# Attention loop of a fused attention, soft-MoE and feed-forward kernel: order of a pair's steps, one q/k buffer, and the slot step of the last batch

## The chip, the cores and the metric

The kernel runs on one core of a Trainium2 chip. Its time is device microseconds, from the runs of the kernel on that core. All data are float32 in memory.

## The reference, cut to what matters

Causal attention over 4 batches, 12 heads, 448 positions and 64 dimensions; its output, as 1792 tokens of 768, goes through a soft mixture of 8 experts with 4 slots each, and that through a feed-forward layer whose activation is h cos h.

```python
# attention: q, k, v are (4, 12, 448, 64)
scores = scale * np.matmul(q, k.transpose(0, 1, 3, 2))
scores = np.where(mask, -1000000000.0, scores)          # causal
scores = scores - np.max(scores, axis=-1, keepdims=True)
attn = np.exp(scores)
attn = attn / (np.sum(attn, axis=-1, keepdims=True) + 1e-09)
x = np.matmul(attn, v)                                   # then (1792, 768)
# soft MoE: phi (768, 32), w1 (8, 768, 1024), w2 (8, 1024, 768)
logits = x @ phi
d = exp(logits - logits.max(0)); d /= d.sum(0) + 1e-09   # over all tokens
slot_input = d.T @ x                                     # (32, 768)
for e in range(8):
    slot_out[e] = np.maximum(slot_input[e] @ w1[e], 0.0) @ w2[e]
c = exp(logits - logits.max(1)); c /= c.sum(1) + 1e-09   # over the 32 slots
y = c @ slot_out
# feed-forward: w_in (768, 2048), w_out (2048, 768)
h = y @ w_in
out = (h * np.cos(h)) @ w_out
```

## The kernel before

It has three stages. The first runs attention and the slots' softmax; the second runs the experts on the 32 slot rows and streams all of `w1` and `w2`; the third is the feed-forward layer, laid out by a planner at build time. The change touches the first stage and the way from it into the second.

**Pairs and iterations.** Two heads make a pair; a batch has 6 pairs, the kernel `NPAIR` = 24. `pair_step(t)` (line 450) is one iteration of a software pipeline, called for t = 0 to 27 under `tc.manual_schedule()`. There the order of instructions on each engine is the order of the program text; numbers of `PRI` act only outside such blocks. Iteration t computes the scores and exponentials of pair t, transposes the normalised scores of pair t-1 and multiplies them with the values, and transposes the result x of pair t-2.

**One pair.** The scores of a head are split in query blocks: c = 0 (448 key columns), 1 (320), 2 (192) and 3 (64 columns, both heads' last block together). `qk_mm` (line 284, matmuls at L292 and, for c = 3, L287) writes c = 0 of head j to bank j, c = 1 and 2 to bank 2 + j, and c = 3 to the last 64 columns of bank 0, an iteration ahead. `score` (L303) adds the mask on VectorE, takes the row minimum and writes to SBUF; the closure it returns is the exponential on ScalarE (L305) with its row sum. `recip` (L312, L313) and `norm` (L322) normalise, on VectorE and GpSimd by `CFG["norm"]`. `t_a` and `t_b` (transposes at L325) turn one head's weights into banks `TA` and `TB`; `ev_t` (L176) copies each bank to SBUF, all four on ScalarE. `pv` (L355 to L368) multiplies with the values into bank `OB`; `ev_o` (L176, `xts<-bank`) copies x out. `x_t` (L376) transposes x into bank `TA`, and `ev_x` (L178) copies that to `xk` on VectorE.

**Slot work of a batch b.** With bo = t - 6b: `phi_round` in iterations 5 and 7 adds up the slots' logits of six pairs in bank `MB` (L387), and `be_logits` (L392) copies them out. In iteration 8 `be_rep` (L396) spreads them over partitions, `be_d` (L401 to L411) makes the running softmax over tokens, `be_dk` transposes it (L325, L417), and `be_u(b, 0)` (L439, L445) adds the first three pairs' part of d.T x to `uacc`. In iteration 9 `be_tok` (L422 to L432) makes the softmax over slots and `be_u(b, 1)` adds the other three pairs. So the slot work falls on t mod 6 = 5, 1, 2 and 3 once the first batch is done.

**From the loop to the experts.** For the last batch `be_u(3, 0)` is in t = 26 and `be_u(3, 1)` in t = 27. After the loop, outside the manual block, `uacc` is scaled by the softmax's sum (L571 to L573), six matmuls with `rep` (L575) make `slotT` (L576), and the expert loop begins (matmuls at L733 and L748). `be_tok(3)` is written inside the expert loop; the scheduler may place it.

**Buffers and loads.** Large SBUF tiles come from a ring of `NSLOT` = 26 slots of 1 MB: two q/k buffers of two pairs each, two of scores, `pts`, `xts`, two `xk`, and the rest for pieces of the experts' weights, of which there are 48. All loads are issued on SP in program order, and SP waits there until the target is free. At the end of iteration t come `load_raw(t + 3)` for q and k, `load_v(t + 1)`, and up to 18 weight pieces, one in most iterations; `CFG["PL"]` adds pieces from t = 21 on as slots of the attention stage come free. The expert loop issues a further piece for each that it has read. Values of odd pairs lie in the end of an `xk` slot, of even pairs in others.

Of the kernel before, what the change touches and what calls it, by code (L numbers as in the profile page):

```python
# [27 lines left out]
NSLOT = 26  # L28
# [3 lines left out]
LD = False  # L32
CFG = {'rm': 2,
        'PL': {21: 1, 23: 2, 24: 2, 25: 1, 27: 2},
        'ev': 'AAAA',
# [118 lines left out]
def moe_stack_kernel(ctx: ExitStack, tc: tile.TileContext, qk, v, cst, phi, w1, w2, w_in, w_out, out):  # L154
# [36 lines left out]
    qks = [slot(f"qk{i}") for i in range(2)]  # L191
# [3 lines left out]
    xks = [slot(f"xk{i}") for i in range(2)]  # L195
# [26 lines left out]
    def QK(p):  # L222
        return qks[p // 2 % 2][:, (p % 2) * 960:(p % 2) * 960 + 960]
# [126 lines left out]
    @pr(lambda i: f"ev{i}")  # L350
    def ev_t(i):
        copy(CFG["ev"][i], PT(i), (TA, TB)[i % 2])

# [65 lines left out]
    @pr("tok")  # L419
    def be_tok(b):  # L420
        for r in range(4):
            PE.matmul(MB[0:112, 128 + 32 * r:160 + 32 * r], lhsT=ltr[:, 112 * r:112 * r + 112], rhs=rep[:, 0:32],  # L422
                      start=True, stop=True)
# [4 lines left out]
        ACT.activation(ek, ek, AF.Exp)  # L428
        DVE.tensor_reduce(st[0:112, 20:24], ek, axis=AX.X, op=ALU.add)
# [4 lines left out]
    @pr("u")  # L434
    def be_u(b, half):
        for i in range(3):
            p = b * NPB + 3 * half + i
            for r in range(4):
                PE.matmul(MB[32 * r:32 * r + 32, 128 * i:128 * i + 128], lhsT=dk[0:112, r, :], rhs=XK(p)[:, r, :],  # L439
                          start=True, stop=True)  # L440
        u = uacc[:, 384 * half:384 * half + 384]
        if b == 0:
            DVE.tensor_copy(u, MB[:, 0:384])
        else:
            DVE.scalar_tensor_tensor(u, u, st[:, 9:10], MB[:, 0:384], op0=ALU.mult, op1=ALU.add)  # L445


    NPRE = NSLOT - 8

    def pair_step(t):  # L450
# [7 lines left out]
        def sc(j, c, p=t):  # L458
            if p < NPAIR:
                ex[j, c] = score(p, j, c)  # L460

        def e(j, c):
            if (j, c) in ex:
# [52 lines left out]
        if 8 in bo:  # L516
            be_dk(bo[8])
        if prv:
            pv(p1)
# [12 lines left out]
        if 9 in bo:  # L532
# [16 lines left out]
    with tc.manual_schedule():  # L549
        load_raw(0)  # L550
        SP.dma_start(cs, cst)
        load_raw(1)
        load_v(0)
        SP.dma_start(phs, phi)
        load_raw(2)
# [7 lines left out]
        for t in range(NPAIR + 4):  # L563
# [3 lines left out]
    slotT = phs  # L567
# [3 lines left out]
    DVE.tensor_scalar(st[:, 40:41], st[:, 11:12], 1e-9, None, op0=ALU.add)  # L571
    DVE.reciprocal(st[:, 41:42], st[:, 40:41])
    DVE.tensor_scalar(uacc, uacc, st[:, 41:42], None, op0=ALU.mult)  # L573
    for i in range(6):
# [465 lines left out]
```

## Time and profile before

| | us |
|---|---|
| median of 3 runs | 581.81 |
| lowest, highest | 581.11, 583.5 |
| the profiled execution | 580.56 |
| its span, first to last instruction | 578.8 |
| first scores of the first pair | 5.42 |
| first scores of the last pair | 194.86 |
| first expert matmul | 223.73 |

The profile is that of one execution, with times in us from the span's start. PE is TensorE's matmuls, PEld its weight loads, DVE VectorE, ACT ScalarE, POOL GpSimd, and SPq the queue on which the loads are issued. A line of a timeline merges instructions of one kind that follow each other; the bracket at its end tells how long the engine was idle before it and what ended that. A line of a stretch has the stretch and its length, each engine's busy time with its count of instructions, the granted clock of TensorE as a share of 2.4 GHz, the DMA engines' busy share and GB/s. Some records of instructions can be missing, so that counts of equal stretches differ a little.

### The profile page before, as it was taken

How to read it: one execution, taken by the hardware profiler on the slowest of the kernel's cores; microseconds unless marked ns; L12 is line 12 of the kernel's file. 1: busy time of each engine (PE TensorE's matmuls, PEld its weight loads, DVE VectorE, ACT ScalarE, POOL GpSimd, SP SyncE). 2: the span in 40 equal slices, each digit the busy share in tenths (PEclk: the TensorE clock that was granted, in tenths of full speed). 3: DMA queues.
4: the chain of work that ended last, by engine and by line, in shares of the span. 5: the costliest groups of instructions: out<-in, count | busy, mean ns of one | idle time of the engine just before them, and what ended most of it. 6: DMA issues, size and time to landing. Idle time of an engine off the chain costs nothing.

```text
span 578.8 us, 10216 instructions
## 1 busy us (share of the span) xinstructions
PE 529.0 (91%) x3772; PEld 379.2 (66%) x3772; DVE 347.0 (60%) x879; ACT 329.9 (57%) x762; POOL 174.8 (30%) x209
## 2 busy tenths in 40 slices
PE   5999989999998969998676999899999999999997
PEld 2666666666666634333164878687877777888997
DVE  4566576657657632300176887799588996534532
ACT  4888768868876831011066666565655745443552
POOL 1332332232233210000024346263533734322231
PEclk9999999999999996999796999999999999999999
DMA  7364716554570896999954143333324210202201
GB/s 242 135 246 174 251 65 240 178 197 180 178 251 24 315 370 253 421 418 421 418 199 163 54 165 109 110 110 109 110 109 171 102 53 5 109 2 109 110 1 54
DMA packets 23953, 100.26 MB, mean 173 GB/s; under 512 B 2656, under 2 KB 6624, under 8 KB 17760
## 3 DMA queue, kind: packets, MB, share of 16 engines
q1 hardware_dynamic: 23904, 99.63, 46.4%
q8 instruction: 29, 0.48, 0.3%
q14 instruction: 20, 0.16, 0.1%
HBM read 94.11 MB, written 5.51 MB: 172 GB/s over the span
## 4 chain that ended last, share of the span: by engine, by line
PE 50%; DMA 17%; ACT 15%; DVE 13%; issue 4%; POOL 1%; SPq 0%; ACTq 0%; DVEq 0%; POOLq 0%
PE bank L831 7%; PE bank L830 7%; DMA w<-in_w_dram 7%; PE bank L832 7%; DMA zraw<-in_w_in_dram 5%; ACT pts L176 5%; PE bank L292 5%; ACT p L305 4%; PE bank L325 4%; DMA zraw<-in_w_out_dram 4%; PE bank L360 3%; PE bank L376 2%; PE bank L362 2%; PE bank L733 2%; DVE zscr L811 2%
## 5 line engine op out<-in xcount | busy, mean ns | idle before, releaser
L830 PE MATMUL bank<-zg,zhl 128*128 128x512 f32 (+1 forms) x384 | 142.9, 372 | 0.0
L831 PE MATMUL bank<-zg,zhl 128*128 128x512 f32 (+1 forms) x384 | 140.7, 366 | 0.5 <-POOL zhl L694 0.5
L832 PE MATMUL bank<-zg,zhl 128*128 128x512 f32 (+1 forms) x384 | 140.2, 365 | 0.0
L823 POOL TENSOR_TENSOR zg<-zscr,zg 128x512 fp32r<-128x512 f32 (+1 forms) x64 | 80.6, 1260 | 146.0 <-ACT zg L820 99.9
L322 POOL TENSOR_SCALAR p<-p,pst 128x320 f32<-128x320 f32 (+3 forms) x120 | 62.1, 534 | 141.5 <-DVE pst L313 102.6
L303 DVE CUSTOM_DVE_ANT_0 p<-bank,cs 128x320 f32<-128x320 f32 (+3 forms) x168 | 68.5, 449 | 44.8 <-PE bank L292 41.3
L305 ACT ACTIVATE p<-p,pst 128x320 f32<-128x320 f32 (+3 forms) x168 | 87.6, 523 | 9.6 <-DVE pst L303 9.2
L830 PEld LDWEIGHTS bank<-zg,zhl 128*128 128x128 f32 x384 | 73.2, 191 | 12.7 <-issue 1.2
L831 PEld LDWEIGHTS bank<-zg,zhl 128*128 128x128 f32 x384 | 73.2, 191 | 12.4 <-POOL zhl L694 0.9
L832 PEld LDWEIGHTS bank<-zg,zhl 128*128 128x128 f32 x384 | 73.1, 190 | 12.0
L176 ACT ACTIVATE pts<-bank 128x512 f32<-128x512 f32 x96 | 56.6, 590 | 33.0 <-PE bank L325 32.8
L325 PEld LDWEIGHTS bank<-cs,p 128*128 128x128 f32 (+1 forms) x456 | 49.6, 135 | 23.9 <-issue 20.8
L811 DVE SCALAR_TENSOR_TENSOR zscr<-zscr,bank 128x512 f32<-128x512 int32 (+1 forms) x64 | 39.4, 616 | 39.6 <-ACT zscr L808 39.1
L325 PE MATMUL bank<-cs,p 128*128 128x128 f32 (+1 forms) x456 | 62.5, 282 | 0.2 <-ACT pts L176 0.2
L814 ACT ACTIVATE zscr<-zscr,b_h 128x512 f32<-128x512 f32 (+1 forms) x64 | 42.7, 667 | 30.4 <-DVE zscr L811 30.3
L292 PE MATMUL bank<-qk 64*128 64x192 f32 (+2 forms) x288 | 53.6, 479 | 3.0 <-DVE pst L303 3.0
L817 DVE TENSOR_TENSOR zscr<-bank,zscr 128x512 f32<-128x512 f32 (+1 forms) x64 | 39.6, 619 | 25.9 <-ACT zscr L814 25.8
L808 ACT ACTIVATE zscr<-bank,b_q 128x512 int32<-128x512 f32 (+1 forms) x64 | 40.2, 629 | 22.6 <-PE bank L804 22.4
L820 ACT ACTIVATE zg<-zscr 128x512 fp32r<-128x512 f32 (+1 forms) x64 | 36.8, 576 | 24.5 <-DVE zscr L817 24.4
L659 ACT ACTIVATE zraw<-zraw 128x768 f32<-128x768 f32 x32 | 29.4, 918 | 33.1 <-DMA zraw<-in_w_in_dram 18.0
L694 POOL TENSOR_TENSOR zhl<-uacc,zhl 128x768 fp32r<-128x768 f32 (+1 forms) x12 | 17.9, 1501 | 97.2 <-ACT zhl L681 97.2
L292 PEld LDWEIGHTS bank<-qk 64*128 64x128 f32 x288 | 24.6, 191 | 18.3 <-issue 5.8
(145 smaller groups left out, 668.6 us busy)
## 6 DMA issues: line engine op xcount, KB each, us to landing
w<-in_w_dram SPq DMA_DIRECT2D x48, 1024.0 KB, 7.5
zraw<-in_w_in_dram SPq DMA_DIRECT2D x16, 768.0 KB, 4.8
zraw<-in_w_out_dram SPq DMA_DIRECT2D x16, 768.0 KB, 4.3
qk<-in_qk_dram SPq DMA_DIRECT2D x24, 480.0 KB, 5.9
xk<-in_v_dram SPq DMA_DIRECT2D x12, 256.0 KB, 2.7
out_dram<-zps SPq DMA_DIRECT2D x8, 256.0 KB, 2.1
xts<-in_v_dram SPq DMA_DIRECT2D x12, 128.0 KB, 2.1
lt<-in_v_dram SPq DMA_DIRECT2D x12, 128.0 KB, 2.3
```

The source lines that it names most:

```text
L176: ACT.activation(o, i, AF.Copy)
L292: PE.matmul(sreg(j, c), lhsT=Q(p)[h, q0:q0 + 128], rhs=K(p)[h, 0:ln], start=True, stop=True)
L303: DVE.tensor_tensor_reduce(out=dst, in0=sb, in1=m, scale=-0.125, scalar=3.0e38, op0=ALU.add, op1=ALU.min, accum_out=st_[:, col:col + 1])
L305: return pr(f"exp{j}{c}")(lambda: ACT.activation(dst, dst, AF.Exp, bias=st_[:, col:col + 1], scale=-1.0, accum_out=st_[:, 8 + col:9 + col]))
L322: ENG[CFG["norm"][3 * j + c if c < 3 else 6]].tensor_scalar(dst, dst, st_[:, 24 + col:25 + col], 0.0, op0=ALU.mult, op1=ALU.add)
L325: PE.transpose(out, src, by)
L811: DVE.scalar_tensor_tensor(y_(s), y_(s).bitcast(I32), -2.0 * math.pi, hb[:, 0:n_(s)], op0=ALU.mult, op1=ALU.add)
L814: ACT.activation(y_(s), y_(s), AF.Sin, bias=b_h, scale=1.0)
L823: eng.tensor_tensor(g_(s)[1], y_(s), g_(s)[0].bitcast(F32), ALU.subtract)
L830: PE.matmul(o, lhsT=wh, rhs=gh, start=first, stop=False)
L831: PE.matmul(o, lhsT=wl, rhs=gh, start=False, stop=False)
L832: PE.matmul(o, lhsT=wh, rhs=gl, start=False, stop=last)
```

## The change

Six things change; the arithmetic stays, but for where a factor is applied.

1. The three score blocks of a pair are matmuls of one run at the front of the iteration; before, the first pair of transposes stood between the first block and the others.
2. x's transposes go to bank `OB`, which the value product of the same iteration then overwrites, and stand ahead of the second head's transposes; those of the last pair come at the end of iteration 25.
3. Of the four evictions the fourth is on VectorE (`ev_t(3, "D")`), and behind the last pair the second too.
4. `be_tok` is cut in two: logits, maximum and exponential at the iteration's front (for the last batch in the expert loop as before), sum and scaling at its end.
5. One q/k buffer of two pairs in place of two; `load_raw(t + 2)` stands behind the scores of t, and 19 pieces load in the loop.
6. In the last batch both halves of u are in t = 26, the second in bank `TB`; the reciprocal sum is multiplied into `rep` instead of `uacc`, and `be_slots` makes the slot rows in two halves inside the loop, which has one iteration less.

```diff
+PL = {23: 2, 24: 2, 25: 1, 26: 2}
...
-        'PL': {21: 1, 23: 2, 24: 2, 25: 1, 27: 2},
-        'ev': 'AAAA',
...
-    qks = [slot(f"qk{i}") for i in range(2)]
+    qks = slot("qk")
...
-    xks = [slot(f"xk{i}") for i in range(2)]
+    xks = [slot(f"xk{i}") for i in (1, 0)][::-1]
...
     def QK(p):
-        return qks[p // 2 % 2][:, (p % 2) * 960:(p % 2) * 960 + 960]
+        return qks[:, (p % 2) * 960:(p % 2) * 960 + 960]
...
-            PE.transpose(TA[0:112, 128 * r:128 * r + 128], XT(p)[:, 112 * r:112 * r + 112], ident)
+            PE.transpose(OB[0:112, 128 * r:128 * r + 128], XT(p)[:, 112 * r:112 * r + 112], ident)
...
-        copy(CFG["evx"], XK(p), TA[0:112].rearrange("p (r f) -> p r f", r=4))
+        copy(CFG["evx"], XK(p), OB[0:112].rearrange("p (r f) -> p r f", r=4))
...
-    @pr("tok")
     def be_tok(b):
+        be_tok1(b)
+        be_tok2(b)
+
+    def be_tok1(b):
...
         ACT.activation(ek, ek, AF.Exp)
+
+    def be_tok2(b):
+        ek = ctok[:, 4 * b:4 * b + 4, :]
         DVE.tensor_reduce(st[0:112, 20:24], ek, axis=AX.X, op=ALU.add)
...
-    @pr("u")
     def be_u(b, half):
+        ub = TB if (b, half) == (NB - 1, 1) else MB
...
-    NPRE = NSLOT - 8
+    NPRE = NSLOT - 7
+
+    slotT = phs
+
+    def be_slots(half):
+
+        for i in range(3 * half, 3 * half + 3):
+            PE.matmul(bank[0][:, 32 * i:32 * i + 32], lhsT=uacc[:, 128 * i:128 * i + 128], rhs=pst[0], start=True, stop=True)
+        if half:
+            DVE.tensor_copy(slotT, bank[0][:, 0:192].rearrange("p (i c) -> p i c", i=NPB))
...
         if now:
-            qk_mm(t, 0)
-        if prv:
-            t_a(p1, 0)
+            for c in range(3):
+                qk_mm(t, c)
+        if t + 2 < NPAIR:
+            load_raw(t + 2)
         sc(0, 0)
-        if prv:
-            ev_t(0)
         if 9 in bo and bo[9] < NB - 1:
-            be_tok(bo[9])
-        if 8 in bo:
-            be_rep(bo[8])
+            be_tok1(bo[9])
         sc(1, 0)
         e(0, 0)
         if prv:
+            t_a(p1, 0)
+            ev_t(0, "A")
             t_b(p1, 0)
-            ev_t(1)
-        if now:
-            qk_mm(t, 1)
-            qk_mm(t, 2)
+            ev_t(1, "A" if now else "D")
+        if 8 in bo:
+            be_rep(bo[8])
+        sc(0, 1)
+        sc(1, 1)
+        e(1, 0)
+        if 8 in bo:
+            be_d(bo[8])
+        sc(0, 2)
+        sc(1, 2)
+        if pr2 and t - 2 < NPAIR - 1:
+            x_t(t - 2)
+            ev_x(t - 2)
         if prv:
             t_a(p1, 1)
-        e(1, 0)
-        sc(0, 1)
-        if prv:
-            ev_t(2)
-        sc(0, 2)
+            ev_t(2, "A")
+            t_b(p1, 1)
+            ev_t(3, "D")
         e(0, 1)
...
         e(0, 2)
...
         if nxt:
             qk_mm(t + 1, 3)
+        if 8 in bo:
+            be_dk(bo[8])
+        if prv:
+            pv(p1)
         if now:
             recip(t, 0)
...
+        if 9 in bo and bo[9] < NB - 1:
+            be_tok2(bo[9])
         if now:
             recip(t, 1)
...
         if 8 in bo:
             be_u(bo[8], 0)
-        if 9 in bo:
+            if bo[8] == NB - 1:
+                DVE.tensor_scalar(st[:, 40:41], st[:, 11:12], 1e-9, None, op0=ALU.add)
+                DVE.reciprocal(st[:, 41:42], st[:, 40:41])
+                DVE.tensor_scalar(pst[0], rep[:, 0:32], st[:, 41:42], None, op0=ALU.mult)
+                be_u(NB - 1, 1)
+                be_slots(0)
+                be_slots(1)
+        if 9 in bo and bo[9] < NB - 1:
             be_u(bo[9], 1)
         if 7 in bo:
             phi_round(bo[7], range(4, NPB))
             be_logits(bo[7])
-        if t + 3 < NPAIR:
-            load_raw(t + 3)
+        if t - 2 == NPAIR - 1:
+            x_t(t - 2)
+            ev_x(t - 2)
         if t + 1 < NPAIR:
             load_v(t + 1)
-        if t >= 1 and t % 4 != 0 and len(pieces) < NPRE:
+        if t >= 1 and t % 6 != 0 and len(pieces) < NPRE:
             load_piece()
...
-        for t in range(NPAIR + 4):
+        for t in range(NPAIR + 3):
             pair_step(t)
```

## Rows read from the trace of the kernel before

**Rows 1.** Stretches: iterations 13 to 16; TensorE, its loads, VectorE, ScalarE, GpSimd, clock, DMA

```profile
108.61:116.79 8.18, 7.98 (x66) 5.13 (x62) 5.40 (x24) 6.91 (x22) 3.47 (x8) 1.00 0.29 94
116.79:127.00 10.21, 9.36 (x89) 6.19 (x88) 5.78 (x25) 7.74 (x23) 2.48 (x6) 1.00 0.51 182
127.00:136.69 9.69, 8.68 (x93) 6.21 (x89) 6.93 (x28) 6.63 (x20) 2.60 (x6) 1.00 0.54 184
136.69:143.99 7.30, 7.10 (x61) 4.98 (x57) 5.01 (x20) 5.58 (x17) 1.78 (x4) 1.00 0.65 247
```

**Rows 2.** TensorE's timeline, end of iteration 15 and iteration 16: start, length, instruction, [idle before]

```profile
133.26 0.65 PE L376 MATMUL bank<-cs,xts 128*112 128x128 f32 x4 [1.01 <-ACT pts L176]
...
136.69 1.02 PE L292 MATMUL bank<-qk 64*128 64x448 f32 x4
137.65 1.20 PE L325 MATMUL bank<-cs,p 128*128 128x128 f32 x9
138.78 1.13 PE L292 MATMUL bank<-qk 64*128 64x320 f32 x8
139.84 1.31 PE L325 MATMUL bank<-cs,p 128*128 128x128 f32 x10
141.35 0.65 PE L376 MATMUL bank<-cs,xts 128*112 128x128 f32 x4 [0.20 <-ACT pts L176]
...
142.10 0.34 PE L357 MATMUL bank<-pts,xts 128*64 128x64 f32 x4
...
143.99 0.65 PE L292 MATMUL bank<-qk 64*128 64x448 f32 x2
```

**Rows 3.** The stretch from the last pair's scores to the first expert matmul

```profile
194.86:223.73 28.87, 22.79 (x193) 15.69 (x189) 12.61 (x41) 12.47 (x31) 4.46 (x9) 0.88 0.88 336
```

**Rows 4.** Stretches of the weights' transfers; the last three numbers are clock, DMA share, GB/s

```profile
218.00:224.00 6.00, 4.82 (x32) 4.24 (x28) 2.50 (x8) 1.59 (x2) 0.00 (x0) 0.50 0.79 320
224.00:228.00 4.00, 4.00 (x28) 0.74 (x24) 1.81 (x9) 0.20 (x1) 0.00 (x0) 0.64 0.32 76
232.00:264.00 32.00, 30.57 (x356) 10.69 (x357) 5.85 (x14) 2.34 (x5) 0.00 (x0) 1.00 1.01 421
```

**Rows 5.** ScalarE's timeline in iteration 11: an eviction, and the end of the second exponential

```profile
95.97 0.58 ACT L176 ACTIVATE pts<-bank 128x512 f32<-128x512 f32 x1
...
98.52 0.19 ACT L305 ACTIVATION_READ_ACCUMULATOR p<-p,pst 128x1 f32 x1
```

**Rows 6.** VectorE's timeline in iteration 11, and one step of the slots' softmax in iteration 15

```profile
98.54 0.69 DVE L178 COPY xk<-bank 112x512 f32<-112x512 f32 x1 [0.70 <-PE bank L376]
99.15 0.16 DVE L312 TENSOR_SCALAR pst<-pst 128x4 f32<-128x4 f32 x1
...
99.92 0.22 DVE L303 CUSTOM_DVE_ANT_0 p<-bank,cs 128x64 f32<-128x64 f32 x1
...
130.36 0.29 DVE L429 TENSOR_REDUCE st<-ctok 112x4 f32<-112x128 f32 x1 [0.38 <-ACT ctok L428]
```

**Rows 7.** TensorE's timeline at the start of iteration 1

```profile
11.53 0.87 PE L292 MATMUL bank<-qk 64*128 64x448 f32 x2 [2.39 <-DVE pst L303]
```

**Rows 8.** The loads of q and k, then the weight pieces of line 250: issue to landing

```profile
DMA to landing us min/median/max: 3.2/5.9/8.0
DMA to landing us min/median/max: 4.9/6.4/17.4
```

**Rows 9.** TensorE's timeline from the last pair's scores to the first expert matmul

```profile
194.86 1.02 PE L292 MATMUL bank<-qk 64*128 64x448 f32 x4
...
209.10 0.65 PE L376 MATMUL bank<-cs,xts 128*112 128x128 f32 x4 [0.64 <-ACT xts L176]
...
215.17 0.86 PE L439 MATMUL bank<-xk,dk 112*32 112x128 f32 x24 [0.38 <-DVE dk L417]
...
219.02 1.70 PE L422 MATMUL bank<-cs,lt 128*112 128x32 f32 x8 [0.74 <-DVE uacc L445]
220.53 2.75 PE L575 MATMUL bank<-cs,uacc 128*128 128x32 f32 x12
223.73 1.03 PE L733 MATMUL bank<-w,phs 128*4 128x512 f32 x4 [0.45 <-DVE phs L576]
```

More of the change, by code (lines that the diff above doesn't have):

```diff
@@ L348, in t_b, with ev_t @@
         tr(TB[:, 128:256], P[:, PO[1] + 128:PO[1] + 256])
-    @pr(lambda i: f"ev{i}")
-    def ev_t(i):
-        copy(CFG["ev"][i], PT(i), (TA, TB)[i % 2])
+    @pr(lambda i, e: f"ev{i}")
+    def ev_t(i, e):
+        copy(e, PT(i), (TA, TB)[i % 2])
     @pr("pv")
@@ L438, in be_u @@
             for r in range(4):
-                PE.matmul(MB[32 * r:32 * r + 32, 128 * i:128 * i + 128], lhsT=dk[0:112, r, :], rhs=XK(p)[:, r, :],
+                PE.matmul(ub[32 * r:32 * r + 32, 128 * i:128 * i + 128], lhsT=dk[0:112, r, :], rhs=XK(p)[:, r, :],
                           start=True, stop=True)
@@ L442, in be_u @@
         if b == 0:
-            DVE.tensor_copy(u, MB[:, 0:384])
+            DVE.tensor_copy(u, ub[:, 0:384])
         else:
-            DVE.scalar_tensor_tensor(u, u, st[:, 9:10], MB[:, 0:384], op0=ALU.mult, op1=ALU.add)
-    NPRE = NSLOT - 8
+            DVE.scalar_tensor_tensor(u, u, st[:, 9:10], ub[:, 0:384], op0=ALU.mult, op1=ALU.add)
+    NPRE = NSLOT - 7
[5 more added lines that the diff above has]
+            DVE.tensor_copy(slotT, bank[0][:, 0:192].rearrange("p (i c) -> p i c", i=NPB))
     def pair_step(t):
@@ L456, in pair_step, with sc @@
         ex = {}
-        def sc(j, c, p=t):
-            if p < NPAIR:
-                ex[j, c] = score(p, j, c)
+        def sc(j, c):
+            if now:
+                ex[j, c] = score(t, j, c)
         def e(j, c):
-            if (j, c) in ex:
+            if now:
                 ex[j, c]()
         if now:
-            qk_mm(t, 0)
-        if prv:
-            t_a(p1, 0)
+            for c in range(3):
+                qk_mm(t, c)
+        if t + 2 < NPAIR:
+            load_raw(t + 2)
         sc(0, 0)
-        if prv:
-            ev_t(0)
         if 9 in bo and bo[9] < NB - 1:
-            be_tok(bo[9])
-        if 8 in bo:
-            be_rep(bo[8])
+            be_tok1(bo[9])
         sc(1, 0)
@@ L515, in pair_step @@
         e(1, 2)
[L516 to L519, printed above, removed]
         if nxt:
             e3()
+        if 9 in bo and bo[9] < NB - 1:
+            be_tok2(bo[9])
         if now:
@@ L536, in pair_step @@
             be_logits(bo[7])
-        if t + 3 < NPAIR:
-            load_raw(t + 3)
+        if t - 2 == NPAIR - 1:
+            x_t(t - 2)
+            ev_x(t - 2)
         if t + 1 < NPAIR:
             load_v(t + 1)
-        if t >= 1 and t % 4 != 0 and len(pieces) < NPRE:
+        if t >= 1 and t % 6 != 0 and len(pieces) < NPRE:
             load_piece()
-        for _ in range(CFG["PL"].get(t, 0)):
+        for _ in range(PL.get(t, 0)):
             load_piece()
-        if t == NPAIR + 1:
+        if t == NPAIR:
             for i in (1, 2):
@@ L551, in moe_stack_kernel @@
         SP.dma_start(cs, cst)
+        load_v(0)
         load_raw(1)
-        load_v(0)
         SP.dma_start(phs, phi)
-        load_raw(2)
         DVE.memset(TB, 0.0)
@@ L562, in moe_stack_kernel @@
         score(0, 0, 3)()
-        for t in range(NPAIR + 4):
+        for t in range(NPAIR + 3):
             pair_step(t)
-    slotT = phs
     hT = dk.rearrange("p c m -> p (c m)").rearrange("p (c m) -> p c m", c=8)
@@ L570, in moe_stack_kernel @@
     so = cs[:, 384:640]
[L571 to L574, printed above, removed]
-        PE.matmul(bank[0][:, 32 * i:32 * i + 32], lhsT=uacc[:, 128 * i:128 * i + 128], rhs=rep[:, 0:32], start=True, stop=True)
-    DVE.tensor_copy(slotT, bank[0][:, 0:192].rearrange("p (i c) -> p i c", i=NPB))
     for i in (4, 5):
```

12 lines of the change are left out of this document (removed).

## The prediction

> **What bounds the kernel now.** I read the iterations of the attention loop first, by stretches, then TensorE's timeline inside them, then the way from the last pair to the first expert matmul with the transfers beside it, and last ScalarE and VectorE inside a plain iteration. Two things bind, one after the other.
>
> In the loop TensorE sets the pace. A plain iteration (t mod 6 = 0 or 4, no slot work) takes 7.30 us, with this engine busy for 7.10; iterations with slot work take 8.18, 10.21 and 9.69 [rows 1]. The timeline shows two leads. The transposes of x start 0.20 us late, for ScalarE's eviction of bank TA. The ten transposes ahead of them take 1.51 us to this successor where nine take 1.13; at that pace ten take 1.26, so 0.25 to 0.35 goes in the wait. And the score matmuls run twice, 448 columns in 0.96 us and 320+192 columns in 1.06 [rows 2]. So 64 columns cost 0.10, and each run costs some 0.26 beside its columns.
>
> Behind the loop a chain of 28.87 us leads from the last pair's first scores at 194.86 to the first expert matmul at 223.73 [rows 3, 9]. From there the weights' transfers bind: the queue moves 421 GB/s in 232 to 264, but only 320 in 218 to 224 and 76 in 224 to 228 [rows 4], since every slot is taken until the first expert piece has been read. What shortens the way to that piece moves all behind it: the experts, and the last stage, which the change doesn't touch.
>
> **The loop, part by part.** Times below count from an iteration's first score matmul.
>
> *Joined scores, x through OB.* One of two runs goes: 0.26 by the rows. A gap of up to 0.1 ahead of the second run goes too. The wait for TA goes: 0.3. Together 0.65; TensorE alone would need 7.30 - 0.65 = 6.65. If joining saves nothing, it is 7.0.
>
> *What is late next.* The last pair's transposes now come behind all scores, at 1.8 instead of 0.96, and the second group ends near 3.0. From there ScalarE's order binds: an eviction, an exponential, an eviction, two exponentials, which take 95.97 to 98.71, 2.74 us [rows 5]. Then VectorE: from its reciprocal's first step at 99.15 over a normalisation to the end of the 64-column score at 100.14, 1.0 [rows 6]. The next score matmul writes the bank that this reads. With 0.15 for three handovers the loop is 3.0 + 2.74 + 1.0 + 0.15 = 6.9. So a plain iteration goes from 7.30 to 6.9 and not to 6.65. That such a wait is real shows at 11.53: the first score matmul sat 2.39 us until VectorE had read its 64 columns, though it writes the other 448 of the bank [rows 7]. The Trainium skill, PSUM — Partial Sum Buffer, section PSUM bank collisions raise a hardware error, says to guard the bank and not the address; by addresses alone the iteration would be 6.65, by the bank it is 6.9, and the row agrees with the page.
>
> *Fourth eviction on VectorE.* A copy of 112x512 out of a bank takes 0.69 there [rows 6], one of 128x512 on ScalarE 0.58 [rows 5]. VectorE is done with the six scores near 3.6, with x's copy at 4.3, with this one at 5.3, and its reciprocal can't start before 5.8: 0.5 of slack hides it. Without that cover it costs up to 0.69 an iteration.
>
> *Added wait: the value product waits for x's copy out of OB.* Behind it on TensorE stands the next iteration. The copy ends at 4.3, the product's turn is at 4.6: I take nothing, bounds 0 and 0.4.
>
> *One q/k buffer.* The load for t+2 moves to the front of iteration t and waits on SP for the third run of scores, at 1.9. Behind it on SP stand the values of t+1 and the weight piece, both due only at the iteration's end. Its data are needed 4.4 into the next iteration, 9.3 us after the issue. Such loads take 3.2 to 8.0 to land, median 5.9 [rows 8]: hidden, with 1.3 left. The freed slot takes a nineteenth piece during the loop.
>
> *Iterations with slot work.* Those with a phi round (t mod 6 = 1 and 5) end on TensorE, later than the 6.9, and lose the 0.65: 8.18 [rows 1] becomes 7.55. In t mod 6 = 2 TensorE is busy for 9.36 of 10.21 [rows 1]; the 0.65 goes, and of the idle 0.85 some 0.55, since the transposes of d still wait for their exponential: 9.0. In t mod 6 = 3 x's transposes waited 1.01 [rows 2]; that goes. But the token logits now stand behind all scores, their VectorE step starts at 2.7 and holds the second score and ScalarE's first exponential; the evictions slip and the value product starts at 6.3. With its 1.89 (142.10 to 143.99, [rows 2]) and 0.86 for u's half [rows 9] the end is 9.05, for 9.69. The second part of that softmax, four steps of up to 0.29 [rows 6], some 1.0, ends the iteration on VectorE and pushes the next first score to 1.9 instead of 1.07: t mod 6 = 4 becomes 7.6, 0.3 longer than before.
>
> Six iterations: 6.9 + 7.55 + 9.0 + 9.05 + 7.6 + 7.55 = 47.65, against 7.30 + 8.18 + 10.21 + 9.69 + 7.30 + 8.18 = 50.86: 3.2 saved. That stands twice whole (t = 6 to 17), 2.6 for t = 18 to 22, and for t = 1 to 5, where slot work is one phi round, 3 x 0.4 + 0.65 + some 0.4 = 2.3. Sum **11.3 us**; 16 if TensorE alone binds, 4 if joining saves nothing and ScalarE's loop stays at 7.3.
>
> **The way to the first expert matmul.** Behind the last pair's scores four evictions stand in a row on ScalarE; with two of them on VectorE two times 0.58 lie beside: 1.2 (0.6 to 1.5). The last transposes of x, 0.65 at 209.10, leave the path: 0.6. From u at 215.17 to the first expert matmul it was 8.56 [rows 9]: u's halves in turn, each with a sum, the scaling of `uacc`, token logits, slots, a copy. It will be u 0.9, a sum 0.6, three small steps that scale `rep` 0.6, slots 2.75, copy and handover 0.55: 5.4, so 3.2 saved; u's second half lies beside it in bank TB. The slots ran at a granted clock of 0.50, the lower level of 1.2 GHz [rows 4]; at the upper they would save 1.4 more. Token logits, 1.70 [rows 9], could stand between slots and experts: up to 1.1 lost beside the copy. Sum **5.0** (3 to 7).
>
> The queue can follow. The first expert matmul comes 28.87 - 5.0 = 23.9 after the last pair's first scores; reading a slot takes about 1.9 and a lone piece 4.9 to land [rows 8], which is 30.7 for piece 26. Pieces 24 and 25, which wait for u, are down by 27. So the 5.0 reaches the stream, and up to 1.7 more if the queue doesn't restart from empty.
>
> **The sum.** 11.3 + 5.0 = 16.3. The profiled execution took 580.56 us, its span 578.8, and lies 1.25 below the median of 581.81. 580.56 - 16.3 = 564.3, on the median's scale 565.5: I say **565**.
>
> **Rivals.** *ScalarE's loop is longer than I count* (late evictions hold it at 7.3, or joining saves nothing): 4 to 5 in the loop, 5 behind it, 572. For it: it is the late next, 0.25 above TensorE. Against: even with the slots' logits it is busy for only 6.91 of 8.18 [rows 1], and it loses an eviction.
> *The gain behind the loop is hidden* by the queue or the token logits: the loop's alone counts, 569. For it: pieces 24 and 25 still wait for u. Against: the 76 GB/s ahead of piece 26.
> *No wait on the 64-column read, and a queue that never runs empty*: plain iterations of 6.65, more behind the loop, 559. Against: [rows 7].
> *The one q/k buffer binds*, and the kernel is slower than before. It decides once a load lands more than 9.3 after its issue; then each iteration grows by the excess. To eat 16.3 over 22 iterations and come out 3 us slower takes 0.9 in each, a landing at 10.2: 585. For it: one landed after 8.0. Against: the median of 5.9.
>
> **How the numbers follow.** Forecast 0.60, ScalarE's loop 0.16, hidden gain 0.11, no bank wait 0.07, q/k buffer 0.04, anything else 0.02. The range takes in the first three and the bounds of both sums, 557 to 575. A measurement of this kernel can tell about 0.5% (2.9 us) from no change. Faster by more: 0.92; within: 0.04; slower: 0.04.
>
> **What would show it.** Plain iterations near 6.9, the first score matmul waiting for VectorE's 64-column read; x's transposes waiting for nobody; slot iterations 0.6 to 1.2 shorter; the last pair's scores near 183.6; the first expert matmul 24 behind them, no stretch of 76 GB/s; the last stage as long as before. Wrong would be: score matmuls waiting for q/k, value products for x's copy, a VectorE that never idles ahead of its reciprocal, or token logits ahead of the experts while the queue runs dry.

## The result, and the profile after

The changed kernel takes 566.89 us (median of 4 runs, 563.26 to 568.7) beside 582.65 for the kernel before on the same chip, a ratio of 0.9715 with an interval of 0.9674 to 0.9756. In a second set it took 567.68 (6 runs, 566.24 to 569.05) beside 583.68 (17 runs), 0.9727 (0.9698 to 0.9755). The forecast was 565, its range 557 to 575.

The profiled execution of after took 568.70 us, 1.8 above the first median, its span 566.8. The profiled execution before (580.56) lies under its later medians. So these two differ by 11.9 where the medians differ by 16; a second profile of after took 566.60. I read both.

In the rows below lines have moved: scores L291, transposes L324, evictions L175 (ScalarE) and L177 (VectorE), VectorE's scores L302, x's transposes L375, u L444, token logits L424, slots L460, first expert matmul L743. These stretches are iterations 12 to 16 of after, columns as in [rows 1]:

```profile
97.14:104.06 6.92, 6.73 (x61) 5.40 (x58) 5.05 (x21) 5.56 (x17) 1.96 (x4) 1.00 0.68 260
104.06:111.60 7.54, 7.54 (x61) 5.55 (x61) 6.16 (x25) 6.48 (x21) 3.21 (x8) 1.00 0.33 103
111.60:121.32 9.72, 8.80 (x89) 6.43 (x87) 6.77 (x27) 7.45 (x23) 2.94 (x7) 1.00 0.53 188
121.32:130.48 9.16, 8.34 (x94) 6.57 (x90) 6.51 (x25) 5.58 (x19) 2.17 (x5) 1.00 0.55 197
130.48:137.59 7.11, 6.82 (x62) 5.17 (x58) 6.25 (x26) 5.15 (x17) 2.18 (x5) 1.00 0.67 255
```

A plain iteration takes 6.92 for 7.30 of [rows 1], and TensorE has gaps in it: 6.73 busy. t mod 6 = 1 takes 7.54 without a gap; t mod 6 = 2 is 9.72 with 8.80 busy, so it waits somewhere. TensorE's timeline of iteration 12, plain, answers [rows 2]:

```profile
97.14 1.89 PE L291 MATMUL bank<-qk 64*128 64x448 f32 x12
98.95 1.20 PE L324 MATMUL bank<-cs,p 128*128 128x128 f32 x9
99.99 0.60 PE L375 MATMUL bank<-cs,xts 128*112 128x128 f32 x4
...
104.06 0.65 PE L291 MATMUL bank<-qk 64*128 64x448 f32 x2 [0.19 <-DVE pst L302]
```

The scores' one run takes 1.81 to its successor where two took 0.96 and 1.06; x's transposes wait for nobody; the one bracket is the next first score matmul waiting for VectorE's 64-column read. VectorE's side of it:

```profile
100.70 0.69 DVE L177 COPY xk<-bank 112x512 f32<-112x512 f32 x1
101.84 0.69 DVE L177 COPY pts<-bank 128x512 f32<-128x512 f32 x1 [0.45 <-PE bank L324]
102.99 0.17 DVE L311 TENSOR_SCALAR pst<-pst 128x4 f32<-128x4 f32 x1 [0.46 <-ACT p L304]
103.78 0.22 DVE L302 CUSTOM_DVE_ANT_0 p<-bank,cs 128x64 f32<-128x64 f32 x1
```

The fourth eviction (101.84) has 0.46 of idle time behind it, until ScalarE's exponential. Where t mod 6 = 2 waits is seen in iteration 14, here on TensorE:

```profile
117.23 0.65 PE L324 MATMUL bank<-cs,dT 128*112 128x128 f32 x4 [0.16 <-ACT dT L406]
118.64 0.34 PE L356 MATMUL bank<-pts,xts 128*64 128x64 f32 x4 [0.76 <-DVE xk L177]
```

And on VectorE at that time:

```profile
117.21 0.22 DVE L410 SCALAR_TENSOR_TENSOR st<-st 128x1 f32<-128x1 f32 x1 [0.98 <-ACT dT L406]
117.35 0.35 DVE L302 CUSTOM_DVE_ANT_0 p<-bank,cs 128x192 f32<-128x192 f32 x1
117.90 0.69 DVE L177 COPY xk<-bank 112x512 f32<-112x512 f32 x1
```

The value product waits 0.76 for x's copy, and that stands on VectorE behind a one-column step (L410) which sat 0.98 until ScalarE had the exponential of d. The loads of q and k (issue to landing, least, median and most, as [rows 8]) got faster, and no score matmul waits for one after the first:

```profile
DMA to landing us min/median/max: 3.2/4.4/6.2
```

Behind the loop, the stretch from the last pair's scores to the first expert matmul, and three stretches of the weights' transfers, answering [rows 3, 4]:

```profile
185.58:211.97 26.39, 23.65 (x188) 17.15 (x189) 14.00 (x43) 9.59 (x26) 4.70 (x10) 0.85 0.85 307
205.00:211.97 6.97, 6.52 (x64) 5.88 (x57) 2.67 (x9) 0.00 (x0) 0.00 (x0) 0.50 0.69 241
212.00:218.00 6.00, 6.00 (x32) 1.08 (x36) 2.25 (x11) 1.80 (x3) 0.00 (x0) 0.54 0.74 277
224.00:228.00 4.00, 4.00 (x48) 1.10 (x44) 3.02 (x6) 0.17 (x1) 0.00 (x0) 1.00 1.01 422
```

TensorE's timeline there, answering [rows 9]:

```profile
204.54 2.79 PE L444 MATMUL bank<-xk,dk 112*32 112x128 f32 x48 [0.38 <-DVE dk L416]
207.26 1.70 PE L424 MATMUL bank<-cs,lt 128*112 128x32 f32 x8
208.77 2.75 PE L460 MATMUL bank<-pst,uacc 128*128 128x32 f32 x12
211.97 2.74 PE L743 MATMUL bank<-w,phs 128*4 128x512 f32 x12 [0.45 <-DVE phs L462]
```

The first expert matmul comes 11.76 sooner than in [rows 9], and no stretch of 76 GB/s is left (in steps of 4 us from 185 to 229 the least is 176 GB/s, in 205 to 209). But from 205 on the granted clock is 0.50, the lower level of 1.2 GHz, and token logits stand ahead of the slots. The same instructions in the second profile of after:

```profile
204.14 2.70 PE L444 MATMUL bank<-xk,dk 112*32 112x128 f32 x48 [0.38 <-DVE dk L416]
206.76 0.97 PE L424 MATMUL bank<-cs,lt 128*112 128x32 f32 x8
207.57 1.50 PE L460 MATMUL bank<-pst,uacc 128*128 128x32 f32 x12
209.53 7.03 PE L743 MATMUL bank<-w,phs 128*4 128x512 f32 x48 [0.45 <-DVE phs L462]
```

From the last pair's scores (185.04 here) it is 24.49, 1.9 less, in the same order: token logits and slots took little more than half, the upper level.

The working of the forecast against the traces (saved us; iterations by the starts of their first score matmuls):

| stretch | forecast | after | second profile of after |
|---|---|---|---|
| first scores and iteration 0 | 0 | -0.85 | -0.36 |
| t = 1 to 5 | 2.3 | 2.03 | 2.05 |
| t = 6 to 17 | 6.4 | 5.86 | 5.89 |
| t = 18 to 22 | 2.6 | 2.24 | 2.24 |
| last scores to first expert matmul | 5.0 | 2.48 | 4.38 |
| from there to the end of the span | 0 | 0.16 | -0.19 |
| sum | 16.3 | 11.9 | 14.0 |

### The profile page after: what moved, and what is told of

Its sections match the earlier page's. It is cut to its first block, busy times and chain, and to the rows that moved or that the text cites. A ratio compares the mean times of both kernels' runs of the same rounds, so it can differ in the third digit from the quotient of the medians.

```text
span 566.8 us, 10260 instructions
## 1 busy us (share of the span) xinstructions
PE 520.8 (92%) x3772; PEld 388.6 (69%) x3772; DVE 362.9 (64%) x904; ACT 318.1 (56%) x737; POOL 175.7 (31%) x209
## 5 line engine op out<-in xcount | busy, mean ns | idle before, releaser
L304 ACT ACTIVATE p<-p,pst 128x320 f32<-128x320 f32 (+3 forms) x168 | 87.6, 526 | 32.8 <-DVE pst L302 30.9
L302 DVE CUSTOM_DVE_ANT_0 p<-bank,cs 128x320 f32<-128x320 f32 (+3 forms) x168 | 66.9, 449 | 16.7 <-PE bank L291 12.6
L324 PE MATMUL bank<-cs,p 128*128 128x128 f32 (+1 forms) x456 | 59.8, 278 | 3.1 <-ACT pts L175 2.9
L324 PEld LDWEIGHTS bank<-cs,p 128*128 128x128 f32 (+1 forms) x456 | 49.6, 134 | 11.3 <-issue 9.6
L291 PE MATMUL bank<-qk 64*128 64x192 f32 (+2 forms) x288 | 48.3, 470 | 5.5 <-DVE pst L302 5.5
L291 PEld LDWEIGHTS bank<-qk 64*128 64x128 f32 x288 | 27.2, 196 | 26.4 <-issue 10.3
L175 ACT ACTIVATE pts<-bank 128x512 f32<-128x512 f32 x71 | 40.5, 591 | 3.9 <-PE bank L324 2.3
```

Of the source, the lines that this page charges most:

```text
L175: ACT.activation(o, i, AF.Copy)
L291: PE.matmul(sreg(j, c), lhsT=Q(p)[h, q0:q0 + 128], rhs=K(p)[h, 0:ln], start=True, stop=True)
L302: DVE.tensor_tensor_reduce(out=dst, in0=sb, in1=m, scale=-0.125, scalar=3.0e38, op0=ALU.add, op1=ALU.min, accum_out=st_[:, col:col + 1])
L304: return pr(f"exp{j}{c}")(lambda: ACT.activation(dst, dst, AF.Exp, bias=st_[:, col:col + 1], scale=-1.0, accum_out=st_[:, 8 + col:9 + col]))
L324: PE.transpose(out, src, by)
```

## The experiments: the parts of the loop

The edits are to the changed kernel, but for the one that makes the same move in the kernel before; all were run beside the kernel before. "Scores" in the table is the start of the last pair's scores, "expert" that of the first expert matmul, both in the profiled execution.

| kernel | median us | ratio to before | plain | t mod 6 = 1, 5 | 2 | 3 | 4 | scores | expert |
|---|---|---|---|---|---|---|---|---|---|
| after, again | 567.68 | 0.9727 (0.9698 to 0.9755) | 6.92 | 7.55 | 9.72 | 9.15 | 7.11 | 185.04 | 209.53 |
| scores split | 574.94 | 0.985 (0.9817 to 0.9882) | 7.26 | 8.15 | 10.12 | 8.84 | 7.26 | 192.83 | 218.75 |
| x through TA | 584.14 | 0.9998 (0.9971 to 1.0025) | 7.54 | 8.42 | 9.98 | 10.02 | 7.54 | 198.70 | 222.91 |
| fourth copy on ScalarE | 573.67 | 0.9823 (0.9783 to 0.9863) | 7.41 | 7.55 | 9.72 | 9.15 | 8.12 | 192.31 | 218.27 |
| 64-column score sooner | 560.56 | 0.9607 (0.9564 to 0.965) | 6.67 | 7.55 | 9.72 | 9.15 | 6.67 | 179.85 | 206.62 |
| d's sum later | 564.94 | 0.9676 (0.9629 to 0.9723) | 6.92 | 7.55 | 8.88 | 9.15 | 7.11 | 183.81 | 210.17 |

**The change as it is.**

> The changed kernel as it is, for the spread of its own runs and a second profile. Its four times lay between 563.26 and 568.7 and its profiled execution was the slowest of them. Theory: the spread lies behind the loop, in how the weights' queue runs, so that in this profile the last pair's scores start again at 185.6 within 0.1 and the first expert matmul at 212.0 within 0.3, while the first matmul of the last stage moves by as much as the time does. Rival: the loop itself varies, by 1 us or more at the last pair's scores. Median 565 to 568 by both.

The loop is steady: every iteration from t = 1 on has the length that it had in the first profile, within 0.03. But the last pair's scores came 0.54 sooner, not within 0.1, nearly all of it at the start and in iteration 0, and the first expert matmul 2.4 sooner, not within 0.3: what varies lies ahead of the experts as well as behind them. The stretch from the first expert matmul to the first matmul of the last stage took 67.4 in one profile and 65.9 in the other, and what follows 287.5 and 289.3.

**Scores in two runs.**

```diff
-            for c in range(3):
-                qk_mm(t, c)
+            qk_mm(t, 0)
...
             ev_t(1, "A" if now else "D")
+        if now:
+            qk_mm(t, 1)
+            qk_mm(t, 2)
```

The load of the next q and k moves behind them too.

> The scores of a pair again in two runs, c = 0 ahead of the last pair's first transposes and c = 1, 2 behind them; the rest as changed. Theory (a run costs some 0.26 beside its columns and 0.1 of gap; joined, the 64-column read of bank 0 binds at 6.9, split, TensorE alone): plain iterations (t mod 6 = 0) 6.92 become 7.0 and lose their wait for VectorE's 64 columns; t mod 6 = 1 and 5, which TensorE sets, go from 7.55 to 7.9; the slot iterations grow by 0.2; the last pair's scores come 4.6 later, at 190.2, the time is 571. Rival 1 (joining saves nothing): 7.55 stays, scores within 1 us of 185.6, 567. Rival 2 (nothing hides the run's cost anywhere): 0.36 in every iteration, 7.3 in a plain one, 193.5, 575.

All but t mod 6 = 3 grow, t mod 6 = 1 and 5 by 0.60 and plain ones by 0.34: near rival 2 by the end (192.83, 574.94), but not by its mechanism. TensorE in a plain iteration of this kernel:

```profile
105.06 1.26 PE L324 MATMUL bank<-cs,p 128*128 128x128 f32 x10
106.80 0.34 PE L356 MATMUL bank<-pts,xts 128*64 128x64 f32 x4 [0.31 <-DVE xk L177]
```

A run more costs 0.21 (0.96 + 1.06 against 1.81), and the later c = 1 and 2 make VectorE's last scores late, behind which x's copy stands: 0.31 of TensorE's time goes in the value product's wait for it. With split scores, the rest of the change (x through OB, the fourth eviction on VectorE) buys almost nothing in a plain iteration (7.26 against 7.30 before).

**x through TA.**

```diff
-            PE.transpose(OB[0:112, 128 * r:128 * r + 128], ...
+            PE.transpose(TA[0:112, 128 * r:128 * r + 128], ...
...
-        if pr2 and t - 2 < NPAIR - 1:
-            x_t(t - 2)
-            ev_x(t - 2)
...
             ev_t(3, "D")
+        if pr2 and t - 2 < NPAIR - 1:
+            x_t(t - 2)
+            ev_x(t - 2)
```

> x's transposes again in bank TA, behind the second head's transposes, and their copy behind the fourth eviction; the rest as changed. The value product then waits for no copy of x. Theory (the wait of the value product for x's copy made t mod 6 = 2 take 9.7 and not 9.0; TA's wait costs 0.2 to 0.3 where TensorE binds): t mod 6 = 2 comes down to 9.2, t mod 6 = 1 and 5 go from 7.55 to 7.8, plain ones from 6.92 to 6.95 to 7.1, last pair's scores 1 to 3 us later, time 568 to 570. Rival 1 (t mod 6 = 2 is long for the transposes of d and not for x's copy): it stays at 9.7. Rival 2 (TA's wait is hidden): 7.55 and 6.92 stay and the scores come 1.5 earlier than 185.6.

The kernel is as slow as before, 14 us more than I expected at most. TensorE in a plain iteration shows two waits for bank TA, not one:

```profile
106.62 1.29 PE L324 MATMUL bank<-cs,p 128*128 128x128 f32 x10 [0.29 <-ACT pts L175]
108.21 0.65 PE L375 MATMUL bank<-cs,xts 128*112 128x128 f32 x4 [0.30 <-ACT pts L175]
```

With all scores at the front the two heads' transposes lie close together, and the second head's wait for the first eviction out of TA; in the change x's four transposes fill that time. So, each time with the rest of the change, joined scores without OB make a plain iteration longer (7.54), OB without joined scores leaves it at 7.26, and both together give 6.92. t mod 6 = 2 takes 9.98 with those two waits in it, which settles nothing about x's copy; "d's sum later" does.

**The fourth copy on ScalarE.**

```diff
-            ev_t(3, "D")
+            ev_t(3, "A")
```

> The fourth eviction again on ScalarE, at the same place of its order; the rest as changed. Theory (ScalarE's chain of evictions and exponentials, then VectorE to the 64-column score, sets a plain iteration): 0.58 more on the chain, plain iterations go from 6.92 to 7.5, t mod 6 = 1 and 5 from 7.55 to 7.6 to 7.9, the last pair's scores 5 to 8 us later, the time 572 to 575. Rival (VectorE's work, not ScalarE's, binds ahead of the 64-column score): plain iterations stay at 6.92 or fall, time 565 to 567.

Plain iterations take 7.41, those set by TensorE stay at 7.55, scores 7.3 later, 573.67: near the theory, which had 7.5 in a plain iteration. That t mod 6 = 4 grows by 1.01 was in no forecast, and its cause stays open. VectorE in a plain iteration:

```profile
107.22 0.17 DVE L311 TENSOR_SCALAR pst<-pst 128x4 f32<-128x4 f32 x1 [2.09 <-ACT p L304]
```

VectorE idles 2.09 ahead of its reciprocal, until ScalarE's exponential (L304) is there. So ScalarE's chain binds, not VectorE's work.

**The 64-column score sooner.** On VectorE alone:

```diff
+        if nxt:
+            e3 = score(t + 1, 0, 3)
         if now:
             recip(t, 0)
             for c in range(4):
                 norm(t, 0, c)
-        if nxt:
-            e3 = score(t + 1, 0, 3)
```

> One step moved on VectorE: the 64-column score of bank 0 stands ahead of the first reciprocal and the normalisation, not behind them; the rest as changed. Theory (the next first score matmul waits for that read of bank 0, 0.18 in the trace of after, and TensorE alone would need 6.74): the wait goes, plain iterations (t mod 6 = 0) go from 6.92 to 6.74, t mod 6 = 4 from 7.11 to 6.9, 1 and 5 stay at 7.55; the last pair's scores 1.5 to 2 us sooner, the time 565 to 566. Rival (the wait only shows what ScalarE's chain sets; the value product or the next transposes are late by as much): 6.92 stays.

A stretch of one plain iteration; TensorE is busy from end to end (columns as in [rows 1]):

```profile
92.81:99.48 6.67, 6.67 (x62) 5.41 (x58) 4.94 (x20) 5.40 (x16) 1.70 (x4) 1.00 0.74 269
```

So the wait for bank 0 was what set the 6.92, and 6.67 is TensorE's own time. It also set the start: iteration 0 went from 6.27 to 5.27. This one move is worth 5.2 at the last pair's scores, of which 1.25 are iteration 1, where the pair's scores ran at the upper clock in this execution (below, "Moves together"); 3.9 are left. The time is 7.1 lower, with intervals that don't touch (0.9564 to 0.965 against 0.9698 to 0.9755). That is more than I expected (6.74, and a time of 565 to 566), and what the time gained beyond the 3.9 is not explained.

**The same move in the kernel before.**

> The kernel before with the one move of s03_sooner: the 64-column score of bank 0 ahead of VectorE's first reciprocal. Theory (before the change TensorE set a plain iteration by itself, and the wait for that read stood only at the start, 0.66 and 2.39; the joined scores made it the next limit): plain iterations stay at 7.30, t mod 6 = 1 at 8.18, iteration 0 goes from 6.11 to 5.0, the last pair's scores from 194.86 to 192.5 to 193.8, the time is 1 to 2.4 shorter, a ratio of 0.996 to 0.998. Rival (the read was a limit before as well): plain iterations of 7.1 or less, last pair's scores under 191, ratio under 0.992.

Plain iterations stay at 7.30, t mod 6 = 1 at 8.18, iteration 0 goes to 5.27; the ratio is 0.9965 (0.9942 to 0.9987), inside the theory's. The last pair's scores came no sooner in its profile (195.18), since the first scores started 0.5 later and iteration 1 took 9.37. So the read was no limit of the steady loop before; the change made it one.

**d's sum later.** The step of L410 moves behind the fourth eviction:

```diff
         ACT.activation(dT, MB[:, 0:448], AF.Exp, ...
+    def be_d2(b):
         if b == 0:
...
             ev_t(3, "D")
+        if 8 in bo:
+            be_d2(bo[8])
```

> One step moved on VectorE: the last small step of the running softmax, which waits for ScalarE's exponential of d, stands behind the fourth eviction, not ahead of the pair's last two scores and x's copy; the rest as changed. Theory (in t mod 6 = 2 that step holds x's copy and with it the value product, 0.76 idle in the trace): that idle time goes, t mod 6 = 2 takes 9.0 to 9.1 in place of 9.72, the others stay, last pair's scores 2 us sooner, the time 565 to 566. Rival (the transposes of d still wait for the exponential and take over): 9.5 to 9.72.

```profile
117.12 0.65 PE L324 MATMUL bank<-cs,dT 128*112 128x128 f32 x4
117.70 0.34 PE L356 MATMUL bank<-pts,xts 128*64 128x64 f32 x4
```

No bracket is left: the value product follows d's transposes, and t mod 6 = 2 takes 8.88. The theory holds in the trace, and the transposes of d don't take over. The last pair's scores came only 1.2 sooner, since iteration 1 took 9.53 in this profile, and the time's interval overlaps the change's own (0.9629 to 0.9723, 0.9698 to 0.9755).

## The experiments: behind the loop

| kernel | median us | ratio to before | u to expert | scores to expert |
|---|---|---|---|---|
| after, first and second profile | 566.89, 567.68 | 0.9715, 0.9727 | 7.43, 5.39 | 26.39, 24.49 |
| token logits behind | 567.34 | 0.9722 (0.969 to 0.9754) | 6.07 | 24.95 |
| gaps filled | 566.38 | 0.9708 (0.9678 to 0.9737) | 4.36 | 24.53 |
| slots as before | 568.03 | 0.9752 (0.9712 to 0.9792) | 9.20 | 28.08 |
| loop steps moved | 558.80 | 0.9591 (0.9556 to 0.9625) | 4.36 | 23.25 |
| all moves | 558.02 | 0.9575 (0.9539 to 0.9611) | 4.19 | 23.07 |

**Token logits behind.**

```diff
             if (g, hf) == (0, 1):
+                PE.transpose(MB[:, 128:256], h1[:, 0:128], ident)
                 be_tok(NB - 1)
```

> The last batch's token logits can't start ahead of the first expert's hidden layer (a transpose of that into their bank is added); the rest as changed. Theory (the token logits stand between u and the slots and are on the path): the slots follow u directly, the first expert matmul comes 0.97 us sooner where the granted clock is at the upper level and 1.7 where it is at the lower, and the last stage starts by as much sooner; time 566 to 566.7. Rival (the weights' queue hides it): last stage's start and time as with the change, 567.6.

```profile
204.00 2.79 PE L444 MATMUL bank<-xk,dk 112*32 112x128 f32 x48 [0.38 <-DVE dk L416]
206.86 2.77 PE L460 MATMUL bank<-pst,uacc 128*128 128x32 f32 x12
210.07 4.27 PE L744 MATMUL bank<-w,phs 128*4 128x512 f32 x20 [0.45 <-DVE phs L462]
```

The slots follow u, and the way from u is 1.36 shorter at the same lower clock. So the logits were on the path. The time doesn't show it: 567.34 against 567.68, inside both intervals. Nor does the start of the last stage settle it: 275.77, for 279.33 and 275.40 in the change's two profiles.

**Gaps filled.** `warm(n)` is n matmuls of `ident` with `ident` into bank 3; here W1 is 14 and W2 is 3:

```diff
         if 8 in bo:
+            if bo[8] == NB - 1:
+                warm(W1)
             be_dk(bo[8])
+            if bo[8] == NB - 1:
+                warm(W2)
```

> 17 matmuls without use into an idle bank, 14 into TensorE's wait for the exponential of d of the last batch (1.85 us) and 3 into its wait for the copy of d's transposes (0.38); the rest as changed. Theory (the run-to-run spread and much of the missing gain behind the loop come from the granted clock, which falls to the lower level once TensorE has idled there: u's halves 2.70 to 2.79 and slots 1.50 to 2.75 as against 1.52 and 1.50 where it didn't fall): the clock stays at 1.00 up to the slots, u takes 1.52, token logits 0.97, slots 1.50, the first expert matmul comes 24.2 to 24.5 behind the last pair's scores in place of 26.4, the last stage starts 1 to 3 us sooner than at 279.3, the time is 564 to 566 and its spread under 3 us. Rival (the clock falls without regard to these gaps): 26.4, 567.6.

```profile
201.04 3.29 PE L467 MATMUL bank<-cs 128*128 128x128 f32 x28
205.36 1.52 PE L445 MATMUL bank<-xk,dk 112*32 112x128 f32 x48
207.77 1.50 PE L461 MATMUL bank<-pst,uacc 128*128 128x32 f32 x12
```

u took 1.52 and the slots 1.50, the upper level. Fourteen such matmuls took 3.29, though, not 1.85, and u began some 1.2 late (20.17 behind the last pair's scores, for 18.96 and 19.10), which ate most of it: 24.53, and a time that can't be told from the change's. Its four times lie within 1.1 us, the change's within 5.4 and 2.8, as the theory has it, but four runs are few. Nor do these two runs with filled gaps (this and "all moves") show that the filling held the clock: without it u's 48 records took 1.52 in two profiles too ("x through TA", "loop steps moved"), 1.86 and 2.28 in two ("scores split", "fourth copy on ScalarE"), and 2.70 or more in the other six of the changed kernel and its variants. And in "all moves" the granted clock was 0.50 from 203 to 206, just behind the first expert matmul (202.09), as in "loop steps moved" from 203 to 205, where no gap was filled. That stays open.

**Slots as before.**

```diff
-        ub = TB if (b, half) == (NB - 1, 1) else MB
+        ub = MB
...
-        for t in range(NPAIR + 3):
+        for t in range(NPAIR + 4):
...
+    DVE.tensor_scalar(uacc, uacc, st[:, 41:42], None, op0=ALU.mult)
+    for i in range(6):
+        PE.matmul(bank[0][:, 32 * i:32 * i + 32], lhsT=uacc[...], rhs=rep[:, 0:32], ...)
```

> The changed kernel with the last batch's slot step as before: u's second half in the next iteration and in the same bank, uacc scaled behind the loop, then the slots. Theory (at the lower clock TensorE's own work is most of the way, so that only the handovers between u's halves and the scaling go): from u to the first expert matmul 8.6 to 9.0 in place of 7.43, first expert matmul 27.5 to 28 behind the last pair's scores in place of 26.4, the time 1 to 1.5 longer. Rival 1 (the step is worth the 3.2 that I counted): 29.5, 570.5. Rival 2 (nothing): 26.4, 567.6.

```profile
204.05 1.51 PE L444 MATMUL bank<-xk,dk 112*32 112x128 f32 x24 [0.38 <-DVE dk L416]
206.29 1.50 PE L444 MATMUL bank<-xk,dk 112*32 112x128 f32 x24 [0.73 <-DVE uacc L450]
208.54 1.70 PE L424 MATMUL bank<-cs,lt 128*112 128x32 f32 x8 [0.74 <-DVE uacc L450]
```

u to expert 9.20, so the new slot step is worth 1.8 at the lower clock: the two brackets of 0.73 and 0.74, and some 0.3 of handovers. That is above the theory and below rival 1. In the time it is 0.35, inside the intervals.

**Moves together.** `loop_steps_moved` has the two moves of VectorE and, at the start, pair 1's q and k ahead of pair 0's values.

```diff
-        load_v(0)
         load_raw(1)
+        load_v(0)
```

> Three moves together on the changed kernel: the 64-column score sooner (as in s03_sooner), the last step of the running softmax later (as in d_sum_later), and at the start the load of pair 1's q and k ahead of pair 0's values, as it was before the change. Theory (each wait is its own, so that the gains add up): plain iterations 6.67, t mod 6 = 2 8.9, first scores at 5.4, the last pair's scores at 177.0 (179.85 less 3 times 0.84 and some 0.3), the time 557.5 to 558.5. Rival (with the iterations before it shorter, t mod 6 = 2 finds its exponential as late as ever): 9.4, 179, 560.

The two moves add up as expected (6.67, 8.88); the order of the loads brought nothing that can be told from the spread of other runs (first scores 5.49). The last pair's scores came at 178.69 and not at 177.0, since iteration 1 took 8.50 here where it took 7.25 in "64-column score sooner": the pair's scores took 3.57 for 1.89, which is the lower clock for the upper. The trace's first record of the clock, at the upper level, begins at 14.72 here and at 9.67 there; ahead of it the rows of a stretch show 1.00 without a record. TensorE's timeline of this kernel:

```profile
10.76 3.57 PE L291 MATMUL bank<-qk 64*128 64x448 f32 x12 [1.08 <-DVE pst L302]
```

And of the other:

```profile
10.71 1.89 PE L291 MATMUL bank<-qk 64*128 64x448 f32 x12 [1.08 <-DVE pst L302]
```

`all_moves` adds the later token logits and 8 matmuls in the gaps.

> The three moves of loop_steps_moved, and behind the loop the token logits kept behind the first expert's hidden layer and 8 matmuls without use in place of 17 in TensorE's two waits (7 and 1). Theory (token logits on the path, clock held up by work in the gaps): first expert matmul 22.5 to 23.5 behind the last pair's scores, u 1.52, slots 1.50, the last stage starts by 1.5 to 3 sooner than in loop_steps_moved, the time is 555 to 557. Rival (the weights' queue hides what the slots gain, as it seemed to in token_logits_behind): the same time as loop_steps_moved within 1 us.

```profile
197.90 1.52 PE L447 MATMUL bank<-xk,dk 112*32 112x128 f32 x48 [0.16 <-DVE dk L419]
200.11 1.52 PE L463 MATMUL bank<-pst,uacc 128*128 128x32 f32 x12 [0.69 <-DVE pst L558]
```

Without the logits the slots wait 0.69 for VectorE's scaled `rep`, so most of what they gave up is idle time now. The stretch is as forecast (23.07), the time is not: 558.02 and 558.80 are the same, as the rival had it, and the last stage began at 269.16, for 267.33 in "loop steps moved". Both beat the change: their intervals (up to 0.9611 and 0.9625) end below its own (from 0.9674).

## Why the forecast was right, point by point

*Joined scores.* The size was near: 0.21 for 0.26. But its two halves aren't a sum of independent terms, as I wrote them. I priced TA's wait at 0.3, from the kernel before, where x's transposes alone met it [rows 2]; behind joined scores it is 0.59 at two places, and the change's order hides both.

*What is late next.* Right: 6.92 for 6.9, with the bracket that I named, and TensorE's own time below it (6.67 for 6.65). The Trainium skill, PSUM — Partial Sum Buffer, section PSUM bank collisions raise a hardware error, says to guard by bank and not by address. The move of the 64-column read agrees with that as far as this program goes: VectorE's score over the other 448 columns began at 98.19 in iteration 12, long before the read at 103.78, and the wait went with the read of the 64. What the chip does without such a guard no run here shows. ScalarE's chain is a limit 0.25 above TensorE, not at 7.3; the rival of 572 is what the fourth copy on ScalarE would have made (573.67).

*Fourth eviction.* Hidden, with 0.46 left where I had counted 0.5.

*The value product's wait for x's copy: the step that failed.* I took nothing, from a plain iteration, where 0.44 was left (100.70 + 0.69 to 101.83). I never looked at it in t mod 6 = 2, where d's sum stands ahead of x's copy on VectorE. It stood there before the change too, and VectorE idled for it, but the copy then read bank TA and the value product did not wait for it. These are rows of iteration 14 in the kernel before:

```profile
123.52 0.22 DVE L411 SCALAR_TENSOR_TENSOR st<-st 128x1 f32<-128x1 f32 x1 [1.22 <-ACT dT L407]
124.12 0.34 PE L357 MATMUL bank<-pts,xts 128*64 128x64 f32 x4
124.35 0.69 DVE L178 COPY xk<-bank 112x512 f32<-112x512 f32 x1
```

With x in OB the product comes behind the copy, and so behind that idle time. It cost 0.76 there, outside my bounds of 0 to 0.4, and is why t mod 6 = 2 takes 9.72 for 9.0 (9.46 in t = 8); the run that took it away gained 0.76 to 0.84 in each of t = 8, 14 and 20.

*Slot iterations.* 7.55 right; t mod 6 = 3 9.15 for 9.05; t mod 6 = 4 7.11 for 7.6: the first score of VectorE slipped by 0.45 against a plain iteration, not by 0.8, so I gave back 0.5 too much, which hid part of the error in t mod 6 = 2.

*The start* isn't in my sum at all: 0.85 lost in one profile, 0.36 in the other. VectorE's score for c = 2 now stands behind the second head's c = 1, so ScalarE's exponential, the reciprocal and the 64-column read come later in iteration 0, which took 6.27 for 6.11 in the second profile. In the first it took 6.46, where the first scores ran 3.56 for 3.35, and they began 0.5 later (5.92), as the constants landed later.

*One q/k buffer.* Hidden: loads landed after at most 6.2, and no score waited. The rival of 585 is out.

*Behind the loop.* From u to the first expert matmul I counted 5.4, with u at 0.9 and the slots at 2.75: one at the upper clock, the other at the lower. At the upper it is 4.36 ("x through TA", "loop steps moved"), at the lower 7.43. And I allowed for token logits only beside the copy, while they took their whole 0.97 to 1.70. Evictions and x's transposes brought 1.2 to 1.35 (20.31 from scores to u in [rows 9], 18.96 and 19.10 after) where I had 1.8. So 5.0 was 2.5 to 4.4: the hidden-gain rival in part, through token logits and clock. On the median's scale that rival is 570.5; my 569 was on the profile's. The queue passed nearly all of it on: where the first expert matmul came 11.8 and 14.2 sooner than before, the last stage began 10.5 and 14.5 sooner (279.33 and 275.40, for 289.87).

*The time* came within 2 to 3 us for two reasons. The misses are small beside 16.3. And the sum starts from 580.56, under the later medians of before (582.6 to 583.9): the medians differ by the 16 that I had summed, the profiles only by 11.9 and 14.0. So the agreement of the medians with the sum is better than that of its terms, and by that much it is luck. What each execution adds by itself (65.2 to 67.4 from the first expert matmul to the last stage, 287.2 to 289.6 from there on, over the profiles of all kernels) is as large as the rest, so that the parts behind the loop are shown in their stretches and not in the time.

## What to carry to other kernels

Where a change makes the tightest engine faster, work out which wait is late next and then move that step too: one instruction's place on VectorE was worth 3.9 us at the last pair's scores, where the whole change was worth 9 to 10, and 7 beside 16 in the time. Check a wait that is hidden in the common iteration in each of the rarer ones, and look there at what stands ahead of the producer on its own queue. Two edits that touch the same bank can be worth nothing without each other and 0.4 of 7.3 together, so price them in the new order, not in the old one.

## What had not been expected of the hardware

The same instructions on an otherwise alike execution ran at either level of TensorE's clock behind the loop: u's 48 records between 2.79 and 1.52, the slots 2.75 and 1.50, after a time in which TensorE had idled 1.85 and 0.38; and 3.57 or 1.89 for the scores of the second pair after an idle time of 1.08. By the Trainium skill, TensorE: Matmul & The Clock Gate, section What's actually happening, the window over which the clock gate judges activity runs freely and doesn't restart when a kernel starts, so that the clock's change comes at varying points. The two profiles of after would fit that, with u at the lower level in both and the slots in one (2.75 and 1.50); no run here shows what the gate counts. A float32 matmul of 128x128 by 128x128 stands as two records, and 14 of them took 3.29.
